# Last slab of the down weight gradient held back behind the last two row blocks, which are computed as a pair

## The chip, the cores and the metric

The kernel runs on one core of a Trainium2 chip. The metric is the device time of one execution in microseconds (us), shown as the median of several runs. A profile is one execution recorded by the hardware profiler. Its engines are called PE (TensorE, matrix products) and PEld (its weight loads), DVE (VectorE), ACT (ScalarE), POOL (GpSimd) and SP (SyncE, which only issues transfers). The execution with the profile has a time of its own, and within it a span from the first instruction to the last.

## The reference

The reference is the forward pass and all gradients of one block of a network. With x of 2048 rows and 1024 columns:

```python
x = A_q
xn = _layernorm(x, axis=-1)
s = _A_ref(xn, A_k, A_v, A_shift_k, A_ssm_k, A_ssm_D)       # xn * (long convolution of (shifted k) * v)
g = _silu(_B_ref(xn, B_w_gate, B_w_up, B_w_down))           # ((xn wg) * (xn wu)) wd
return x + s * g
```

`_A_ref` shifts k by four taps, multiplies by v, convolves along the 2048 rows by Fourier transforms and multiplies by its first argument. `_B_ref` has two projections from 1024 to 3584 columns, their product h, and one projection back, w_down, from 3584 to 1024. The outputs are this sum and the gradients for A_q, A_k, A_v, the taps, the convolution's kernel and its skip weights, w_gate, w_up and w_down. Two of them matter here. The gradient of w_down is h transposed times DBM, where DBM is the gradient behind the projection back; it is 3584 x 1024. The gradient of x (out_1) is the gradient of the two projections, DGU times the transposed w_gate and w_up, plus the part DXNA that comes through the convolution branch, taken back through the layer norm, plus grad_out.

## The kernel before

All products are in bf16 with sums in PSUM. The rows are tiled in 16 blocks of 128 (NB = 16), the 3584 columns in 14 slabs of 256 (NSL = 14). The kernel goes through stages, one after another on PE:

1. Layer norm, the two projections, h (written to DRAM as Hd) and the forward convolution.
2. The projection back and the gate for each row block, which writes DBM, DXNA and DY, the gradient for the convolution, to DRAM.
3. For each slab, the product dh (`dh_half`, L1189) and the weight gradients of w_gate and w_up (`dw_slab`, L1213). The product dgu goes to DRAM as DGd.
4. The gradient of w_down, slab by slab (the loop at L1293, products at L1320): for each slab two halves f of 128 rows, for each half two halves dh of 512 columns, and for each of those 16 matmuls over the row blocks. ACT copies the sums into `wbs` and SP stores it at L1325. The slabs of h are loaded by `load_h` (L1232) into three buffers in turn (HSL, L1247); DBM lies in U10, U8, U4 and U5 (L1246).
5. The gradient of x ("the dx stage", L1340 to L1429). Each row block sums 14 pieces n, 7 of w_gate and 7 of w_up, each of 8 matmuls of 128x512 (`dx_part`, L1340). A piece needs a transposed weight piece WGU[n] (1 MB, `load_wgu`, L1278) and, for each group g of four row blocks, a transposed tile dgut n (0.5 MB in two transfers, `load_dgut`, L1283). Group 0 runs as four row blocks at once, piece by piece; groups 1 to 3 as pairs, but for the last two row blocks, which run one after the other, the last of them in two halves of 512 columns (`parts = 2`, L1422). Behind each row block `ln_backward` (L1360) takes the sums back through the layer norm on DVE and ACT and stores the rows.

Two chains of vector work run beside the matmuls as generators. A pump takes steps from them: each step announces its weight with `yield`, and the pump goes on while the sum of the weights behind it is below the share of the stage that is done. `conv_backward` (L906) is pumped through stages 3 and 4 by `btick` (L1177), and begins with `dy_forward` (L885), which loads DYd by POOL, yields its first weight (L897) and then makes the first transforms on PE (`cmm`, L232). Its share is (bcnt - 10) / 410 of C_TOTAL (L1060); each dh group of 16 matmuls adds 1 to bcnt, each group of a weight gradient 2. What is left is run at once at slab 11 (`bdrain`, L1303). `dk_units` (L1006), the gradient of k and of the taps, is pumped through stage 5 by the count of `dx_part` calls (L1347): 16 units, each with a dkh load on POOL, and two transposed loads kT and dkT (L1020, L1022) on SP, for which each buffer exists once.

The order of the instructions on each engine and queue is set when the kernel is built, by a planner that goes by program order among what it estimates to be ready. With PIN set, the DVE's instructions keep program order. `tc.issue_after(ins)` puts what is issued inside behind `ins` on the same queue: the loads of the later dx pieces (L1387 to L1391) stand behind the last store of stage 4, `wst`. `ld` (L60) issues on SP, `st` and `cld` (L65) on POOL. A queue issues in order; a transfer that waits holds back those behind it.

Of the kernel before, what the change touches and what calls it, by code (L numbers as in the profile page):

```python
# [10 lines left out]
ACT = mybir.ActivationFunctionType  # L11
# [8 lines left out]
def build_kernel(  # L20
# [864 lines left out]
    def dy_forward(xs_, sp, cs, then):  # L885
        def load(ds):
            if ds < 8:
                cld(xs_[ds % 2], DYd[ds])

        def half(ds, i):  # L890
            if ds < 8:
                fwd8_half(xs_[ds % 2], i, sp[i], ps_c3)
            else:
                then[i]()
        load(0)
        load(1)
        yield 4.0  # L897
        half(0, 0)
        half(0, 1)
        for ds in range(8):  # L900
            load(ds + 2)
            X = cs.tile([P, 16, 256], BF16, name="DX")
            yield from fwd8(sp, X, cs, lambda i: half(ds + 1, i))
            st(DYFd[ds], X[:])
# [155 lines left out]
    C_TOTAL = 4.0 + 8 * FWD8_W + 16 * (PROD_W + INV8_W) + 8 * 1.4 + 8 * 2.5  # L1060
# [229 lines left out]

    flush()
    ts = []
    for k in range(NSL):  # L1293
        if k + 2 < NSL:
            load_h(k + 2)
# [16 lines left out]
        if k == 13:  # L1312
            ts.append(load_dgut(0, 5))
        h = hs.pop(k)
        for f in range(2):
            wbs = wo.tile([P, D], BF16, name="wbs")[:]
            for dh in range(2):
                ps = ps_b.tile([P, 512], F32, name="psb")
                for b in range(NB):
                    nc.tensor.matmul(ps[:], h[:, b, f * P:(f + 1) * P], DBM[b // 4][:, b % 4, dh * 512:(dh + 1) * 512],  # L1320
                                     start=(b == 0), stop=(b == NB - 1))
                nc.scalar.copy(out=wbs[:, dh * 512:(dh + 1) * 512], in_=ps[:])  # L1322
                btick(2)
            f0 = k * SLW + f * P
            wst = ld(o_dwd[f0:f0 + P, :], wbs)  # L1325
# [14 lines left out]
    def dx_part(t, i, ps, n, dhs=(0, 1)):  # L1340
        for f in range(4):
            for dh in dhs:
                nc.tensor.matmul(ps[:, dh * 512:(dh + 1) * 512], t[n][:, f, i * P:(i + 1) * P],  # L1343
                                 WGU[n][:, f, dh * 512:(dh + 1) * 512],
                                 start=(n == 0 and f == 0), stop=(n == 13 and f == 3))
        kcnt[0] += 1
        kpump(kcnt[0] / (14.0 * 14))  # L1347
# [3 lines left out]
    def ln_loads(b):  # L1351
        rows = slice(b * P, (b + 1) * P)
        ts_ = []
        for nm_, src in (("dxna_t", DXNAd), ("xn_t", XNd), ("dout_t", grad_out.flatten_outer_dims())):
            t = gl.tile([P, D], BF16, name=nm_, bufs=1)
# [4 lines left out]
    def ln_backward(b, mm, parts=1):  # L1360
# [3 lines left out]
        dxn = gl.tile([P, D], F32, name="dxn", bufs=1)  # L1364
        prod = gl.tile([P, D], F32, name="prod", bufs=1)
        dx_t = gl.tile([P, D], BF16, name="dx_t", bufs=1)
        cols = [slice(h * D // parts, (h + 1) * D // parts) for h in range(parts)]
        sums = gs.tile([P, 2, 2], F32, name="sums")
        for h, cl in enumerate(cols):
            ps = mm(h)  # L1370
            tt(dxn[:, cl], ps, dxna_t[:, cl], ADD)
            nc.scalar.activation(dx_t[:, cl], dxn[:, cl], ACT.Identity, accum_out=sums[:, 0, h:h + 1])  # L1372
            tt(prod[:, cl], dxn[:, cl], xn_t[:, cl], MUL)
            nc.scalar.activation(dx_t[:, cl], prod[:, cl], ACT.Identity, accum_out=sums[:, 1, h:h + 1])
        if parts == 2:
            tt(sums[:, :, 0], sums[:, :, 0], sums[:, :, 1], ADD)
        negm = gs.tile([P, 2], F32, name="negm")
        pinned(V.tensor_scalar(negm[:], sums[:, :, 0], -1.0 / D, None, op0=MUL))
        for cl in cols:
            nc.scalar.activation(prod[:, cl], xn_t[:, cl], ACT.Identity, bias=negm[:, 0:1], scale=negm[:, 1:2])  # L1380
            tt(dxn[:, cl], dxn[:, cl], prod[:, cl], ADD)
            pinned(V.scalar_tensor_tensor(dx_t[:, cl], dxn[:, cl], RSTN[:, b:b + 1], dout_t[:, cl], op0=MUL, op1=ADD))
            if parts == 1:
                ln_loads(b + 1)
            (st if parts == 1 else ld)(out_1.flatten_outer_dims()[rows, cl], dx_t[:, cl])

    for n in range(6, 14):  # L1387
# [11 lines left out]
    for i in range(4):  # L1399
# [5 lines left out]
        with tc.high_priority(40):  # L1405
            ln_backward(i, lambda h: pss[i][:])
    for g in range(1, 4):
        for b in (4 * g, 4 * g + 2):
            if b == NB - 2:
                break  # L1410

            pss = [ps_x.tile([P, D], F32, name="psx") for i in range(2)]
            for n in range(14):
                for i in range(2):
                    dx_part(ts, b % 4 + i, pss[i], n)
                if b % 4 == 2:
                    ts[n] = load_dgut(g + 1, n)
            for i in range(2):
                with tc.high_priority(40):
                    ln_backward(b + i, lambda h: pss[i][:])  # L1420
    for b in (NB - 2, NB - 1):
        parts = 2 if b == NB - 1 else 1  # L1422

        def mm(h):
            ps = ps_x.tile([P, D], F32, name="psx")
            for n in range(14):
                dx_part(ts, b % 4, ps, n, (h,) if parts == 2 else (0, 1))
            return ps[:, h * 512:(h + 1) * 512] if parts == 2 else ps[:]
        ln_backward(b, mm, parts)  # L1429
    kdrain()  # L1430
# [65 lines left out]
```

## Time and profile before

| | us |
|---|---|
| median of 11 runs | 1982.79 |
| lowest and highest of them | 1971.18, 2000.29 |
| the profiled execution's time | 1970.73 |
| its span | 1968.6 |
| its PE, DVE, ACT, POOL busy | 1936.3, 1511.7, 647.9, 359.7 |
| stage 4, up to its last matmul | about 1571.5 |
| dx stage, first to last matmul | 1572.1 to 1959.1 |

A busy time is the sum of an engine's instructions and not a limit by itself: what ends the span is the chain of waits. A row of the chain or of a timeline has a start, a length in us, the engine, the written tile, the line and a count. A row of the waits reads: who waited, for whom, us in total, times, the longest. A row of windows gives the stretch, its length, the busy time of PE, PEld, DVE, ACT and POOL with counts, the granted PE clock as a share of full speed, the share of the DMA engines and GB/s. SPq in a timeline is SP issuing a transfer, not the transfer itself. The time of one matmul in a list (379 ns for 128x512) includes its passage through the array, in which the next one overlaps.

### The profile page before, as it was taken

Reading aid. Unit: us, or ns where it says so; the run is one execution under the profiler, and the core shown is the slowest. Engines: PE = TensorE matmul, PEld = TensorE weight load, DVE = VectorE, ACT = ScalarE, POOL = GpSimd, SP = SyncE. Lnnn points to the kernel's source line nnn. Section 1 sums busy time; section 2 is a strip of 40 time slices with the busy share of each in tenths; the row PEclk is TensorE's granted clock in tenths of the full one; section 3 lists DMA queues with packets and bytes.
Section 4 is the critical chain, followed back from the end, with each engine's and each line's share of the span. In section 5 each row is a group of like instructions: output and inputs, shape, how many; then the busy total and the mean of one; then the engine's idle time right before and its main releaser. Section 6 shows DMA issues by size and latency. Waiting matters only on the chain.

```text
span 1968.6 us, 27524 instructions
## 1 busy us (share of the span) xinstructions
PE 1936.3 (98%) x11084; PEld 1041.9 (53%) x11084; DVE 1511.7 (77%) x1687; ACT 647.9 (33%) x954; POOL 359.7 (18%) x526
## 2 busy tenths in 40 slices
PE   7999999999999999999999999999999999999998
PEld 4455555555544446666566666664444444444443
DVE  8689999999626555888899889999996341566764
ACT  5665555555432223333222222222222100211113
POOL 3322213211212221000122112021121100111111
PEclk9999999999999999999999999999999999999999
DMA  7885857666799989565778899566796989989992
GB/s 262 272 269 200 284 198 242 202 213 220 256 292 304 280 264 300 203 208 203 257 231 266 181 276 311 203 241 213 163 302 161 158 191 199 211 168 182 187 167 70
DMA packets 452095, 443.37 MB, mean 225 GB/s; under 512 B 282624, under 2 KB 370488, under 8 KB 438144
## 3 DMA queue, kind: packets, MB, share of 16 engines
q1 hardware_dynamic: 390976, 228.93, 46.3%
q0 software_dynamic: 44672, 183.33, 29.2%
q10 hardware_dynamic: 16320, 29.36, 4.0%
q8 instruction: 86, 1.41, 0.3%
q14 instruction: 41, 0.34, 0.0%
HBM read 192.96 MB, written 189.83 MB: 194 GB/s over the span
## 4 chain that ended last, share of the span: by engine, by line
PE 77%; DVE 10%; issue 7%; DMA 2%; POOL 2%; ACT 1%; SPq 0%; POOLq 0%; DVEq 0%; ACTq 0%
PE psx L1343 20%; PE psb L1217 19%; PE psg L610 10%; PE psb L1320 10%; PE psb L1200 9%; PE psbm L1069 3%; PE psF L232 3%; DVE W L210 2%; DVE KX L210 2%; DVE U L210 2%; DVE HX L210 1%; DVE m L210 1%; PE psY L445 1%; PE psY L997 1%; PE psY L434 1%
## 5 line engine op out<-in xcount | busy, mean ns | idle before, releaser
L610 PE MATMUL psg<-wslab,U 128*128 128x512 bf16 x1792 | 409.3, 380 | 4.4 <-ACT gut L612 2.6
L1217 PE MATMUL psb<-U,U 128*128 128x512 bf16 x1792 | 397.2, 379 | 0.0
L1343 PE MATMUL psx<-U,dgut 128*128 128x512 bf16 x1536 | 333.2, 379 | 0.7 <-ACT wbs L1322 0.7
L1343 PEld LDWEIGHTS <-dgut 128*128 128x128 bf16 x1792 | 175.3, 98 | 212.4 <-issue 1.0
L1217 PEld LDWEIGHTS <-U 128*128 128x128 bf16 x1792 | 175.2, 98 | 197.7
L610 PEld LDWEIGHTS <-U 128*128 128x128 bf16 x1792 | 172.7, 98 | 193.1 <-issue 8.2
L1200 PE MATMUL psb<-wdt,U 128*128 128x256 bf16 x1792 | 206.3, 273 | 1.1 <-ACT bm L1087 1.1
L1320 PE MATMUL psb<-U,U 128*128 128x512 bf16 x896 | 194.4, 379 | 0.0
L1200 PEld LDWEIGHTS <-U 128*128 128x128 bf16 x1792 | 175.6, 98 | 32.1 <-issue 1.4
L612 ACT CAST gut<-psg 128x512 bf16<-128x512 f32 x216 | 126.4, 586 | 181.9 <-PE psg L610 178.8
L1069 PE MATMUL psbm<-U,ht 128*128 128x512 bf16 x784 | 169.9, 379 | 0.0
L1222 ACT CAST wb<-psb 128x512 bf16<-128x512 f32 x112 | 65.6, 586 | 312.0 <-PE psb L1217 301.0
L210 DVE TENSOR_TENSOR W<-W 128x1024 f32<-128x1024 f32 (+1 forms) x144 | 145.9, 1031 | 3.0
L1320 PEld LDWEIGHTS <-U 128*128 128x128 bf16 x896 | 87.5, 98 | 104.5
L1372 ACT ACTIVATE dx_t<-dxn 128x1024 bf16<-128x1024 f32 (+1 forms) x17 | 17.1, 1007 | 328.5 <-DVE dxn L210 243.7
L1069 PEld LDWEIGHTS <-ht 128*128 128x128 bf16 x784 | 76.6, 98 | 91.8
L210 DVE TENSOR_TENSOR U<-U,dht 128x2048 bf16<-128x2048 bf16 x56 | 68.3, 1221 | 50.3 <-ACT dht L1202 50.2
L1202 ACT CAST dht<-psb 128x512 bf16<-128x512 f32 x112 | 65.7, 586 | 120.3 <-PE psb L1200 118.0
L1048 DVE SCALAR_TENSOR_TENSOR dkp<-dkT,kT 128x1024 bf16<-128x1024 bf16 (+2 forms) x64 | 78.3, 1224 | 17.4 <-DMA dkT<-DKSHd 15.6
L1322 ACT CAST wbs<-psb 128x512 bf16<-128x512 f32 x56 | 32.8, 586 | 159.6 <-PE psb L1320 146.9
L210 DVE TENSOR_TENSOR W<-SP 128x1024 f32<-128x1024 f32 x64 | 74.3, 1218 | 6.0 <-ACT SP L254 5.3
L210 DVE TENSOR_TENSOR HX<-W 128x1024 bf16<-128x1024 f32 x64 | 74.9, 1218 | 0.4
(216 smaller groups left out, 2327.0 us busy)
## 6 DMA issues: line engine op xcount, KB each, us to landing
U<-GUd SPq DMA_DIRECT2D x28, 1024.0 KB, 8.7
DGd<-U SPq DMA_DIRECT2D x28, 1024.0 KB, 4.6
GUd<-gut ACTq DMA_DIRECT2D x54, 512.0 KB, 5.7
out_dram<-wb SPq DMA_DIRECT2D x112, 128.0 KB, 4.4
U<-Hd SPq DMA_DIRECT2D x14, 1024.0 KB, 5.9
Hd<-hN POOLq DMA_DIRECT2D x54, 256.0 KB, 4.7
HTd<-hT POOLq DMA_DIRECT2D x54, 256.0 KB, 4.1
ht<-HTd SPq DMA_DIRECT2D x7, 1536.0 KB, 9.5
```

Of the source, the lines that this page charges most:

```text
L210: pinned(V.tensor_tensor(o, a, b, op))
L232: mm = nc.tensor.matmul(ps[:, k].rearrange("p (c d) -> p c d", c=2), T[:, r, k, :], xr[:, r], start=(n == 0), stop=(n == len(rs) - 1 and ( ...
L610: gu_mm[0] = nc.tensor.matmul(ps[:], XNT[q][:, dc, qi * P:(qi + 1) * P], w[:, dc].rearrange("p a f -> p (a f)"), start=(dc == 0), stop=(dc ...
L612: nc.scalar.copy(out=gut[:, :, i], in_=ps[:].rearrange("p (a f) -> p a f", a=2))
L1048: ins = V.scalar_tensor_tensor(prod[:].rearrange("p r d -> p (r d)")[:, lo:H], dkT[:, 0, lo:H], 1.0, kT[:, 0, 13 + m + lo:13 + m + H], op0 ...
L1069: nc.tensor.matmul(ps[:, dh * 512:(dh + 1) * 512], ht(fc)[:, i * P:(i + 1) * P], WD[fc // 4][:, fc % 4, dh * 512:(dh + 1) * 512], start=(f ...
L1200: nc.tensor.matmul(ps[:, x * SLW:(x + 1) * SLW], DBMT[2 * hf + g][:, dc, (b % 4) * P:(b % 4 + 1) * P], wdt[:, dc, :], start=(dc == 0), sto ...
L1202: nc.scalar.copy(out=dht[:, 2 * e:2 * e + 2].rearrange("p b f -> p (b f)"), in_=ps[:])
L1217: nc.tensor.matmul(ps[:], XN[b // 4][:, b % 4, dc * P:(dc + 1) * P], dgus[b // 8][:, :, b % 8], start=(b == 0), stop=(b == NB - 1))
L1222: nc.scalar.copy(out=wb[:, dc % 2].rearrange("p a f -> p (a f)"), in_=ps[:])
L1320: nc.tensor.matmul(ps[:], h[:, b, f * P:(f + 1) * P], DBM[b // 4][:, b % 4, dh * 512:(dh + 1) * 512], start=(b == 0), stop=(b == NB - 1))
L1343: nc.tensor.matmul(ps[:, dh * 512:(dh + 1) * 512], t[n][:, f, i * P:(i + 1) * P], WGU[n][:, f, dh * 512:(dh + 1) * 512], start=(n == 0 and ...
```

## The change

Stage 4 ends after slab 12, and the 13th is computed at the very end. The last two row blocks run as a pair like the others, with twelve pieces together, then pieces 12 and 13 for one block and for the other, and the layer norm of each behind them. While this pair runs, DBM is loaded again into buffers that its pieces 0 to 3 leave, the last slab of h into the buffer of piece 4, and the inputs of the last layer norm into tiles of dgut that are free. The last layer norm has tiles of its own in the places of dgut 0 to 5 (`own`). Then come the 64 matmuls of slab 13, into PSUM tiles of the dx stage and `wbs` tiles in the places of the dk units' tiles, which are therefore run to their end first (`kdrain`); each half of 512 columns is stored by SP as soon as it is copied. The dk pump's share is counted over 13 row blocks instead of 14. The loads of dgut 5, which were issued at slab 13 of stage 4, go into the loop behind `wst`. `ln_backward` no longer has a form in two parts, and its output tile has two buffers. Apart from that, the first weight of `dy_forward` is 7.0 instead of 4.0, also in C_TOTAL.

```diff
--- before.py
+++ after.py
@@ -894,7 +894,7 @@
                 then[i]()
         load(0)
         load(1)
-        yield 4.0
+        yield 7.0
         half(0, 0)
         half(0, 1)
         for ds in range(8):
@@ -1057,7 +1057,7 @@
         st(o_dshk.rearrange("(c p) j -> p c j", p=P), dsko[:])
     DK_TOTAL = 3 + 16 * 7
 
-    C_TOTAL = 4.0 + 8 * FWD8_W + 16 * (PROD_W + INV8_W) + 8 * 1.4 + 8 * 2.5
+    C_TOTAL = 7.0 + 8 * FWD8_W + 16 * (PROD_W + INV8_W) + 8 * 1.4 + 8 * 2.5
     bpump, bdrain = make_pump(conv_backward(), C_TOTAL)
 
     ddo = const.tile([P, 8], BF16, name="ddo")
@@ -1288,10 +1288,15 @@
             nc.sync.dma_start_transpose(out=t[:, 2 * i:2 * i + 2], in_=DGd[2 * j + i, a, 512 * g:512 * g + 512, :])
         return t
 
+    def dwd_mm(ps, h, f, dh):
+        for b in range(NB):
+            nc.tensor.matmul(ps, h[:, b, f * P:(f + 1) * P], DBM[b // 4][:, b % 4, dh * 512:(dh + 1) * 512],
+                             start=(b == 0), stop=(b == NB - 1))
+
     flush()
     ts = []
-    for k in range(NSL):
-        if k + 2 < NSL:
+    for k in range(NSL - 1):
+        if k + 2 < NSL - 1:
             load_h(k + 2)
         with tc.issue_after(wst.ins) if k > 0 else nullcontext():
             if k in (2, 3, 4, 5, 6):
@@ -1309,16 +1314,12 @@
         if k == 12:
             load_wgu(6, gw.tile([P, 4, D], BF16, name="W1")[:])
             ts.append(load_dgut(0, 4))
-        if k == 13:
-            ts.append(load_dgut(0, 5))
         h = hs.pop(k)
         for f in range(2):
             wbs = wo.tile([P, D], BF16, name="wbs")[:]
             for dh in range(2):
                 ps = ps_b.tile([P, 512], F32, name="psb")
-                for b in range(NB):
-                    nc.tensor.matmul(ps[:], h[:, b, f * P:(f + 1) * P], DBM[b // 4][:, b % 4, dh * 512:(dh + 1) * 512],
-                                     start=(b == 0), stop=(b == NB - 1))
+                dwd_mm(ps[:], h, f, dh)
                 nc.scalar.copy(out=wbs[:, dh * 512:(dh + 1) * 512], in_=ps[:])
                 btick(2)
             f0 = k * SLW + f * P
@@ -1337,14 +1338,14 @@
     kpump, kdrain = make_pump(dk_units(kw_), DK_TOTAL)
     kcnt = [0]
 
-    def dx_part(t, i, ps, n, dhs=(0, 1)):
+    def dx_part(t, i, ps, n):
         for f in range(4):
-            for dh in dhs:
+            for dh in range(2):
                 nc.tensor.matmul(ps[:, dh * 512:(dh + 1) * 512], t[n][:, f, i * P:(i + 1) * P],
                                  WGU[n][:, f, dh * 512:(dh + 1) * 512],
                                  start=(n == 0 and f == 0), stop=(n == 13 and f == 3))
         kcnt[0] += 1
-        kpump(kcnt[0] / (14.0 * 14))
+        kpump(kcnt[0] / (14.0 * 13))
 
     ln_in = {}
 
@@ -1352,39 +1353,39 @@
         rows = slice(b * P, (b + 1) * P)
         ts_ = []
         for nm_, src in (("dxna_t", DXNAd), ("xn_t", XNd), ("dout_t", grad_out.flatten_outer_dims())):
-            t = gl.tile([P, D], BF16, name=nm_, bufs=1)
+            t = gl.tile([P, D], BF16, name=nm_, bufs=1) if b < NB - 1 else own(nm_, BF16, len(ts_))
             cld(t[:], src[rows, :])
             ts_.append(t)
         ln_in[b] = ts_
 
-    def ln_backward(b, mm, parts=1):
+    def own(nm_, dt, n):
+        return (gd2 if n < 4 else gd).tile([P, D], dt, name=nm_ + "l", tag=f"dgut{n}")
+
+    def ln_backward(b, ps):
 
         rows = slice(b * P, (b + 1) * P)
         dxna_t, xn_t, dout_t = ln_in.pop(b)
-        dxn = gl.tile([P, D], F32, name="dxn", bufs=1)
-        prod = gl.tile([P, D], F32, name="prod", bufs=1)
-        dx_t = gl.tile([P, D], BF16, name="dx_t", bufs=1)
-        cols = [slice(h * D // parts, (h + 1) * D // parts) for h in range(parts)]
-        sums = gs.tile([P, 2, 2], F32, name="sums")
-        for h, cl in enumerate(cols):
-            ps = mm(h)
-            tt(dxn[:, cl], ps, dxna_t[:, cl], ADD)
-            nc.scalar.activation(dx_t[:, cl], dxn[:, cl], ACT.Identity, accum_out=sums[:, 0, h:h + 1])
-            tt(prod[:, cl], dxn[:, cl], xn_t[:, cl], MUL)
-            nc.scalar.activation(dx_t[:, cl], prod[:, cl], ACT.Identity, accum_out=sums[:, 1, h:h + 1])
-        if parts == 2:
-            tt(sums[:, :, 0], sums[:, :, 0], sums[:, :, 1], ADD)
+        if b < NB - 1:
+            dxn = gl.tile([P, D], F32, name="dxn", bufs=1)
+            prod = gl.tile([P, D], F32, name="prod", bufs=1)
+            dx_t = gl.tile([P, D], BF16, name="dx_t", bufs=2)
+        else:
+            dxn, prod, dx_t = own("dxn", F32, 3), own("prod", F32, 4), own("dx_t", BF16, 5)
+        sums = gs.tile([P, 2], F32, name="sums")
+        tt(dxn[:], ps, dxna_t[:], ADD)
+        nc.scalar.activation(dx_t[:], dxn[:], ACT.Identity, accum_out=sums[:, 0:1])
+        tt(prod[:], dxn[:], xn_t[:], MUL)
+        nc.scalar.activation(dx_t[:], prod[:], ACT.Identity, accum_out=sums[:, 1:2])
         negm = gs.tile([P, 2], F32, name="negm")
-        pinned(V.tensor_scalar(negm[:], sums[:, :, 0], -1.0 / D, None, op0=MUL))
-        for cl in cols:
-            nc.scalar.activation(prod[:, cl], xn_t[:, cl], ACT.Identity, bias=negm[:, 0:1], scale=negm[:, 1:2])
-            tt(dxn[:, cl], dxn[:, cl], prod[:, cl], ADD)
-            pinned(V.scalar_tensor_tensor(dx_t[:, cl], dxn[:, cl], RSTN[:, b:b + 1], dout_t[:, cl], op0=MUL, op1=ADD))
-            if parts == 1:
-                ln_loads(b + 1)
-            (st if parts == 1 else ld)(out_1.flatten_outer_dims()[rows, cl], dx_t[:, cl])
-
-    for n in range(6, 14):
+        pinned(V.tensor_scalar(negm[:], sums[:], -1.0 / D, None, op0=MUL))
+        nc.scalar.activation(prod[:], xn_t[:], ACT.Identity, bias=negm[:, 0:1], scale=negm[:, 1:2])
+        tt(dxn[:], dxn[:], prod[:], ADD)
+        pinned(V.scalar_tensor_tensor(dx_t[:], dxn[:], RSTN[:, b:b + 1], dout_t[:], op0=MUL, op1=ADD))
+        if b < NB - 2:
+            ln_loads(b + 1)
+        st(out_1.flatten_outer_dims()[rows, :], dx_t[:])
+
+    for n in range(5, 14):
         with tc.issue_after(wst.ins):
             if n > 6:
                 load_wgu(n, u8((6, 3, 11, 10, 8, 4, 5)[n - 7], a=4))
@@ -1403,31 +1404,41 @@
             for n in (12, 13):
                 ts[n] = load_dgut(1, n)
         with tc.high_priority(40):
-            ln_backward(i, lambda h: pss[i][:])
+            ln_backward(i, pss[i][:])
     for g in range(1, 4):
         for b in (4 * g, 4 * g + 2):
-            if b == NB - 2:
-                break
-
+            end = b == NB - 2
             pss = [ps_x.tile([P, D], F32, name="psx") for i in range(2)]
-            for n in range(14):
+            for n in range(12 if end else 14):
                 for i in range(2):
                     dx_part(ts, b % 4 + i, pss[i], n)
-                if b % 4 == 2:
+                if end and n < 4:
+                    DBM[n] = u8((7, 0, 1, 9)[n], a=4)
+                    ld(DBM[n], DBMd[512 * n:512 * n + 512, :].rearrange("(b u) d -> u b d", u=P))
+                if end and n == 4:
+                    h = u8(2, "p (b f) -> p b f", b=NB)
+                    ld(h, Hd[NSL - 1])
+                if end and n == 8:
+                    ln_loads(NB - 1)
+                if b % 4 == 2 and not end:
                     ts[n] = load_dgut(g + 1, n)
+            if end:
+                kdrain()
             for i in range(2):
+                if end:
+                    for n in (12, 13):
+                        dx_part(ts, b % 4 + i, pss[i], n)
                 with tc.high_priority(40):
-                    ln_backward(b + i, lambda h: pss[i][:])
-    for b in (NB - 2, NB - 1):
-        parts = 2 if b == NB - 1 else 1
-
-        def mm(h):
-            ps = ps_x.tile([P, D], F32, name="psx")
-            for n in range(14):
-                dx_part(ts, b % 4, ps, n, (h,) if parts == 2 else (0, 1))
-            return ps[:, h * 512:(h + 1) * 512] if parts == 2 else ps[:]
-        ln_backward(b, mm, parts)
-    kdrain()
+                    ln_backward(b + i, pss[i][:])
+    for f in range(2):
+        ps = ps_x.tile([P, D], F32, name="psx")
+        wbs = kw_.tile([P, D], BF16, name="wbs", tag=("dka", "dkp")[f])
+        f0 = (NSL - 1) * SLW + f * P
+        for dh in range(2):
+            hs_ = slice(dh * 512, (dh + 1) * 512)
+            dwd_mm(ps[:, hs_], h, f, dh)
+            nc.scalar.copy(out=wbs[:, hs_], in_=ps[:, hs_])
+            ld(o_dwd[f0:f0 + P, hs_], wbs[:, hs_])
     for p_ in (ps_x, kw_, gs, gl, gd2, ub, ua, gd, gw):
         p_.release()
 
```

## The prediction

> **What bounds the kernel now.** The page comes first: TensorE is busy almost throughout, so only its idle time and the work behind its last matmul can be won.
>
> ```profile
> PE 1936.3 (98%) x11084; PEld 1041.9 (53%) x11084; DVE 1511.7 (77%) x1687; ACT 647.9 (33%) x954; POOL 359.7 (18%) x526
> ```
>
> The chain that ended last, read from 1500 us on, gives the rate and the tail (columns: start, length, what).
>
> ```profile
> 1572.12 387.02 PE psx L1343 x1792
> 1959.14 0.02 issue
> 1959.16 0.70 DVE dxn L210
> ...
> 1964.79 0.75 DVE dx_t L1382
> ```
>
> The dx stage is one unbroken run: 387.02 / 1792 = 0.216 us a matmul. After its end at 1959.14 the layer norm of the last row block stands alone, then a store, up to the span's end at 1968.6: 9.46 us without a matmul.
>
> The waits of TensorE between 770 and 1530 us, and the windows around the one they hold, show the second loss.
>
> ```profile
> PE psF L232 <- DMA A<-DYd: 3.2, 1, 3.2
> 776.00:780.00 4.00, 3.92 (x22) 2.93 (x22) 0.87 (x1) 2.13 (x3) 0.00 (x0) 0.59 0.81 305
> ```
>
> The reader sees one wait of 3.16 us for the first load of DYd (it ended at 776.08) and a granted clock of 0.59 over the next 4 us, which loses 0.41 x 4 = 1.6 us more.
>
> Last, SP's queue from 1523 to 1660 us and the weight loads' waits from 1640 to 1700 us. This is where the moved slab stands now.
>
> ```profile
> 1535.45 22.39 SPq L1288 DMA_TRANSPOSE dgut<-DGd  x3
> 1558.09 1.67 SPq L1020 DMA_TRANSPOSE kT<-in_A_k_dram  x1
> 1560.43 1.22 SPq L1022 DMA_TRANSPOSE dkT<-DKSHd  x1
> ...
> 1578.62 1.16 SPq L1020 DMA_TRANSPOSE kT<-in_A_k_dram  x1
> 1579.83 1.29 SPq L1022 DMA_TRANSPOSE dkT<-DKSHd  x1
> 1581.21 0.53 SPq L61 DMA_DIRECT2D out_dram<-wbs  x1
> ...
> 1591.84 0.57 SPq L61 DMA_DIRECT2D out_dram<-wbs  x1
> 1592.52 2.65 SPq L1288 DMA_TRANSPOSE dgut<-DGd  x2
> 1595.21 11.75 SPq L1281 DMA_TRANSPOSE U<-in_B_w_up_dram  x1
> ...
> 1651.73 8.95 SPq L1288 DMA_TRANSPOSE dgut<-DGd  x6
> ```
> ```profile
> PEld L1343 <- DMA dgut<-DGd: 0.4, 1, 0.4
> ```
>
> The loads of the dx stage (pieces 6 to 13) start only at 1592.52, because SP's queue holds the slabs' stores behind kT loads, which wait for DVE. The 13th piece came 0.4 us late (TensorE went on at 1657.65). So this stream has no slack today, and nobody sees it because slab 13 covers its first 13.8 us.
>
> **Part 1: the slab moves.** 2 x 2 x 16 = 64 matmuls, 64 x 0.216 = 13.8 us, leave the place between the slabs and the dx stage and come back behind it: sum 0. Its Hd load (1 MB) moves too, and the four DBM pieces (1 MB each) are loaded a second time. In the last pair a piece takes 2 x 8 x 0.216 = 3.46 us, so these five are released 3.5 to 17.3 us into the pair and needed 48.4 us in (14 x 3.46). A Hd load lands in 5.7 us (median; 21.7 at worst here): hidden, with 9 us over at the worst; without that cover one load costs 5.7. No transposes are then queued on SP: the pump is finished at 13 row blocks instead of 14, and DVE had finished its last step of it at 1921.1, right behind that count.
>
> **Part 2: the end.** Now: 9.46. Then: after the last matmul an ACT copy of 128x512 (0.59), about 0.05 to start the store, 1.7 for its landing (the SP stores of dx_t, 128 KB, median), 1.3 from that landing to the span's end (1967.28 to 1968.6): 3.7. The layer norms must fit beside the slab. A full one took 7.8 (1921.01 to 1928.79). DVE's order is pinned, so that of block 15 runs behind that of block 14: 15.6 after block 14's sums, and its POOL store lands 3.1 to 3.4 after issue: some 19.2. The slab's last store lands 3.46 + 13.8 + 0.65 + 1.7 = 19.6 after the same point. The two nearly tie; I take the slab, and leave 1 us for the other. ACT's copies queue behind the norms' activations, but each of the slab's two tiles has its own PSUM buffer, so no matmul waits. **Gain 5.8, bounds 4.8 and 6.0.**
>
> **Part 3: first step 7.0 instead of 4.0.** The backward pump stands at bcnt 14 when it now takes the first transform (4 x 636.8/410 = 6.2 > 4). With 7.0 it needs bcnt 15 (5 x 639.8/410 = 7.8). Between lies one group of 16 dh matmuls of 128x256: half of the 32 that the chain gives 3.49, so 1.75. The load itself is issued by POOL at 763.44 behind a store, and does not move. The wait shrinks from 3.16 to 1.4. The clock: waits of 2.6 at L610 and 1.1 at L1200 are in the list of waits, and the granted clock stays at 1.0 there, so I take it that 1.4 does not lower it: 1.6 more. **Gain 3.35; bounds 1.75 (the clock drops anyway) and 4.8 (the wait goes wholly).** DVE does not take it back: the last inverse transform's input was ready at 1509.6 and TensorE took it at 1521.15, 11.6 later.
>
> The Trainium skill (TensorE: Matmul & The Clock Gate, HAM oscillation — how this bites in real kernels) asks for no idle gaps above about 3.4 us. The 0.59 behind a wait of 3.16 disagrees; by the page the drop would not come from this wait, and the part would be worth 1.75, the sum 7.5.
>
> **Part 4: the start of the dx stage.** TensorE needs every piece 13.8 earlier. Piece 5 goes from before the kT loads into the stream: 2.65 longer. Before: 1657.65 - 1592.52 = 65.1 from the stream's start to the last piece. Needed at 1657.26 - 13.8 = 1643.4, so the stream must start by 1643.4 - 65.1 - 2.65 = 1575.7; if the first weight load, 11.75, takes the 4.3 to 5.6 of its sisters, by 1582.7. When does it start? SP's order behind piece 4: kT and dkT of unit 0, two stores, kT and dkT of unit 1, a store, kT and dkT of unit 2, slab 12's last store. The two transposes of piece 5, 7.36 of the 22.39 above, are gone, so dkT issues at 1560.43 - 7.4 = 1553.0 and lands 3.2 later; unit 0's four products take 5.05 (1563.66 to 1568.7), unit 1 takes 10.0 (1568.6 to 1578.6), then 3.2 as now until the store is out: 1553.0 + 3.2 + 5.05 + 10.0 + 3.2 = 1574.5. That is 1.2 before the limit. **Cost 0.** Bounds: a gain of 0.4 (today's late piece); a loss, if the stream starts as late as now, of 1592.5 - 1575.7 = 16.8. The nearest row is the queue's order itself, so I take 0.
>
> The Trainium skill (DMA: Bandwidth & Descriptors, Latency and other measured facts) gives DMA transposes 261 GB/s: an estimate of 6.0 us for a piece of 1.5 MB. Measured: six pieces from 1607.00 to 1651.73, 7.45 each, against TensorE's 6.9; by the page the stream would win 0.9 a piece and leave part 4 with 10 us of slack, the sum unchanged.
>
> **Sum.** 5.8 + 3.35 + 0 = 9.1 us, against the profiled execution's 1970.73: 1961.6. That execution lies 12.1 below the median of the runs shown; I carry the difference over: 1982.8 - 9.1 = 1973.7. From the rows I cannot say where the other runs lose their 12; a stretch like 1536 to 1549, where the DMA queues moved 10 GB/s on average, is a candidate, and the Hd load of slab 13 landed 21.7 after 1535.02, at 1556.7, 0.9 before its matmuls began.
>
> **Rivals.**
> - *The stream comes late (the other side).* At the start of the dx stage TensorE waits for a piece. Price: start minus 1575.7. With one more kT unit ahead it is 1584.5: 8.9, and the sum is -0.2, no change. With the start of now it is 16.8, plus 1.6 of lowered clock as behind the wait at 772.9: 9.3 slower, 1992. It decides from a start at 1584.8 on, 9.1 later than the limit. For it: no slack today, transposes that crawl. Against: two transposes fewer ahead of the chain, one kT unit fewer before the last store.
> - *More is gained.* Slab 13's narrow Hd load and today's late pieces cost the usual run more than the profiled one; both are relieved. 5.8 + 4.8 + 0.4 = 11.0, and up to 5.7 more for a Hd load that misses: 1966 to 1972. For it: the 12 us between profile and median. Against: no row shows that wait.
> - *Part 3 does nothing.* POOL's load lands later, or the transform keeps its place: only 5.8, 1977. For it: the load's landing is decided by DMA traffic. Against: it is issued by the same queue at the same point.
>
> **How the numbers follow.** The measurement of this kernel tells about 0.5% (9.9 us) from no change, and the sum lies just inside it. Sum case 0.41, split by its bounds (6.6 to 11.2) in half: 0.21 faster, 0.20 same. More gained 0.19, faster. Part 3 nothing 0.12, same. Late stream 0.28: 0.13 same, 0.15 slower. Together faster 0.40, same 0.45, slower 0.15. The likeliest case's own range is 1971 to 1977; the range of 8 in 10 goes from 1964 (all of the second rival, and 2 us more for the two medians' own spread) to 1992 (the first rival).
>
> **What would show it.** The last matmul ends some 3.7 us before the span's end and belongs to the slab; a copy and an SP store follow. The wait for A<-DYd is about 1.4, and no window behind it shows a clock under 0.9. The first store-then-transpose of the dx stream lies about 16.9 us after the last slab's matmuls (1574.5 against 1557.6); no wait for dgut or U appears in the dx stage. Wrong: a wait of several us on dgut or U, a POOL store that ends the span, kT loads between the last slab store and its forerunner, or slower transposes.

## The result, and the profile after

The change made the kernel slower: a median of 1999.28 us over 12 runs (1985.18 to 2004.99) against 1981.26 over 47 runs of the kernel before, a ratio of 1.0088, 95% interval 1.0067 to 1.0108. By the ratio that is 17 us lost, where 9 had been forecast as won.

The profiled execution of after took 2003.48 us, its span is 2001.7; against the 1968.6 of before the two spans differ by 33.1. The profile of after lies 4.2 above its median and that of before 10.5 below its own, so the two traces show the loss larger than it usually is. The working below accounts for the 33.1, and the experiments put a price with an interval on the cause.

The page of after, its row of engines and its row of TensorE in 40 slices of 50 us:

```profile
PE 1944.7 (97%) x11084; PEld 1042.4 (52%) x11084; DVE 1510.9 (75%) x1682; ACT 646.6 (32%) x949; POOL 355.5 (18%) x527
...
PE   7999999999999999999999999999999985999999
```

TensorE has as many matmuls as before and is busy 8.4 us longer, and two slices, from some 1600 to 1700 us, now have holes. The waits of TensorE over the whole span of after name what it waited for there:

```profile
PE psx L1344 <- DVE dxn L210: 22.8, 2, 17.3
PE psx L1344 <- DMA dgut<-DGd: 6.3, 5, 4.6
...
PE psF L232 <- DMA A<-DYd: 4.0, 1, 4.0
```

The largest is new in kind. Two times, 17.3 and 5.5 us, the dx stage stood still for DVE to read the sums of a row block out of PSUM into `dxn` (after's timeline of TensorE from 1640 to 1715 us; in brackets: idle before, and what ended it):

```profile
1651.71 14.69 PE L1344 MATMUL psx<-U,dgut 128*128 128x512 bf16 x56 [4.62 <-DMA dgut<-DGd]
1683.71 3.57 PE L1344 MATMUL psx<-U,dgut 128*128 128x512 bf16 x8 [17.31 <-DVE dxn L210]
1692.78 18.01 PE L1344 MATMUL psx<-U,dgut 128*128 128x512 bf16 x72 [5.50 <-DVE dxn L210]
```

Group 0 holds four of these PSUM tiles, and the first pair of group 1 needs two of them back. What DVE did in that time, in after's timeline of DVE from 1585 to 1700 us:

```profile
1589.71 0.69 DVE L210 TENSOR_TENSOR dka<-dka,dkp 128x1024 bf16<-128x1024 bf16 x1
1675.35 1.23 DVE L1048 SCALAR_TENSOR_TENSOR dkp<-dkT,kT 128x1024 bf16<-128x1024 bf16 x1 [84.95 <-DMA dkT<-DKSHd]
...
1682.44 1.22 DVE L210 TENSOR_TENSOR dxn<-psx,dxna_t 128x1024 f32<-128x1024 f32 x1
...
1691.51 1.22 DVE L210 TENSOR_TENSOR dxn<-psx,dxna_t 128x1024 f32<-128x1024 f32 x1
```

DVE was idle for 84.95 us. It waited for the transposed load dkT of the fourth dk unit (unit 3, counted from 0). Its order is pinned, and in that order unit 3 comes ahead of the layer norms of group 0, so their first read of PSUM stood at 1682.44 behind a load that had nothing to do with them. In before the same read came as soon as TensorE had the sums, with only the last of unit 3's products behind it (before's timeline of DVE from 1655 us):

```profile
1658.78 1.22 DVE L210 TENSOR_TENSOR dxn<-psx,dxna_t 128x1024 f32<-128x1024 f32 x1 [61.06 <-PE psx L1343]
...
1666.53 1.22 DVE L1048 SCALAR_TENSOR_TENSOR dkp<-dkT,kT 128x1024 bf16<-128x1024 bf16 x1
```

Why the load was late is in SP's queue, after's timeline of SP from 1520 to 1720 us:

```profile
1572.63 1.16 SPq L1020 DMA_TRANSPOSE kT<-in_A_k_dram  x1
1573.88 1.25 SPq L1022 DMA_TRANSPOSE dkT<-DKSHd  x1
1575.18 1.04 SPq L61 DMA_DIRECT2D out_dram<-wbs  x2
1576.27 9.24 SPq L1288 DMA_TRANSPOSE dgut<-DGd  x4
1585.61 11.91 SPq L1281 DMA_TRANSPOSE U<-in_B_w_up_dram  x1
...
1647.99 22.15 SPq L1288 DMA_TRANSPOSE dgut<-DGd  x16
1670.24 1.24 SPq L1020 DMA_TRANSPOSE kT<-in_A_k_dram  x1
1671.54 1.48 SPq L1022 DMA_TRANSPOSE dkT<-DKSHd  x1
```

The loads of units 0, 1 and 2 are ahead of the stream of the dx stage, that of unit 3 is behind it, and behind seven dgut tiles of group 1 as well (16 transfers, of which the first two are group 0's last tile): it is issued at 1670.24, 94 us behind the stream's start at 1576.27. In before unit 3's kT was issued just ahead of the stream's start at 1592.52 (before's timeline of SP):

```profile
1588.72 1.16 SPq L1020 DMA_TRANSPOSE kT<-in_A_k_dram  x1
```

Standing still also cost clock. After's windows over the gap and over the rest of the dx stage:

```profile
1640.00:1710.00 70.00, 42.30 (x165) 17.13 (x164) 26.16 (x34) 10.62 (x15) 6.81 (x12) 0.78 1.01 201
1710.00:1983.00 273.00, 273.00 (x1266) 123.77 (x1265) 168.35 (x234) 40.33 (x58) 42.32 (x71) 1.00 0.76 167
```

The 165 matmuls of the first window take 42.30 us instead of 165 x 0.216 = 35.6, with a granted clock of 0.78 on average: 6.7 more. By the timeline of TensorE above, some 2.5 of it stand behind the wait of 4.62 for dgut (56 matmuls in 14.69 us instead of 12.1), the rest behind the two waits for dxn.

The end of after is as the change means it to be; its chain that ended last:

```profile
1692.78 290.82 PE psx L1344 x1336
1983.61 10.37 PE psx L1293 x48
...
1994.64 3.63 PE psx L1293 x16
...
1998.29 0.58 ACT wbs L1440
```

The last matmul ends at 1998.25 and the span at 2001.7, 3.45 later, where before had 9.46. Between the two rows of slab matmuls lie 0.67 us for the copy of an earlier tile. The end thus wins 9.46 - 3.45 - 0.67 = 5.3.

Put together: the dx stage starts at 1558.99 instead of 1572.12 (13.1 earlier: the 13.8 of slab 13, less 0.7 that the way up to it lost). It takes 424.5 instead of 387.0, 37.4 more: 22.8 for dxn, 6.3 for dgut, 6.7 of clock, and 1.6 that is left over, about what the stage loses to small waits of weight loads before 1646 us. From its last matmul to the span's end it is 18.3 instead of 9.5, 8.8 more, which is the slab and its wait less the 6.0 at the end. -13.1 + 37.4 + 8.8 = 33.1.

### The profile page after: what moved, and what is told of

Its sections match the earlier page's. It is cut to its first block, busy times and chain, and to the rows that moved or that the text cites. A ratio compares the mean times of both kernels' runs of the same rounds, so it can differ in the third digit from the quotient of the medians.

```text
span 2001.7 us, 27536 instructions
## 1 busy us (share of the span) xinstructions
PE 1944.7 (97%) x11084; PEld 1042.4 (52%) x11084; DVE 1510.9 (75%) x1682; ACT 646.6 (32%) x949; POOL 355.5 (18%) x527
## 5 line engine op out<-in xcount | busy, mean ns | idle before, releaser
L1217 PE MATMUL psb<-U,U 128*128 128x512 bf16 x1792 | 397.4, 379 | 0.0
L1344 PE MATMUL psx<-U,dgut 128*128 128x512 bf16 x1536 | 341.0, 384 | 30.1 <-DVE dxn L210 22.8
L1293 PE MATMUL psb<-U,U 128*128 128x512 bf16 x832 | 180.6, 379 | 0.0
L1376 ACT ACTIVATE dx_t<-dxn 128x1024 bf16<-128x1024 f32 x15 | 15.9, 1057 | 363.9 <-DVE dxn L210 234.9
```

The lines of the kernel that those rows point to most:

```text
L1217: nc.tensor.matmul(ps[:], XN[b // 4][:, b % 4, dc * P:(dc + 1) * P], dgus[b // 8][:, :, b % 8], start=(b == 0), stop=(b == NB - 1))
L1293: nc.tensor.matmul(ps, h[:, b, f * P:(f + 1) * P], DBM[b // 4][:, b % 4, dh * 512:(dh + 1) * 512], start=(b == 0), stop=(b == NB - 1))
```

## The experiments

Three theories stood after this, and a fourth, D, comes with its run. A: DVE's pinned order holds the norms behind unit 3, whose load the stream has overtaken on SP; without that, the other terms of the prediction's sum hold. B: the stream itself is late (dgut), which is the rival on record, and the wait for dxn only follows. C: the pump's new divisor, 13 row blocks instead of 14, brings unit 3 forward in DVE's order. The short diffs are against after, unless another kernel is named; all ratios are against before on the same chip, with 95% intervals.

**Unit 3 held behind the norms.** The pump may not begin unit 3 until the four row blocks of group 0 are through. Loads keep their order on SP, and only DVE's order changes.

```diff
-        kpump(kcnt[0] / (14.0 * 13))
+        part = kcnt[0] / (14.0 * 13)
+        kpump(min(part, 24.0 / DK_TOTAL) if kcnt[0] <= 56 else part)
```

> The changed kernel, with one condition more on the dk pump: it stands still at 24 (behind unit 2) until the four layer norms of group 0 are issued, so that unit 3 stands behind them in DVE's order instead of ahead. Theory A (DVE's fixed order: unit 3 waits for its kT and dkT, which SP now issues behind the dx stream and eight pieces of the next group, and the four norms, whose first read frees the sums' buffers, wait behind unit 3): TensorE's wait for dxn, 22.8 us in the changed kernel's profile, falls under 2, the two low stretches of the clock behind it go too, and the kernel is 0.2 to 0.6% faster than before. Theory B (the stream of transposed loads is what is late; the wait for dxn only follows from it): the waits for dgut grow instead and the time stays 0.6 to 0.9% above before. Theory C (the dk pump counted over 13 row blocks brings too much vector work into the stage): some gain, but the wait for dxn stays over 8 us, since the units are only shifted.

0.9957 (0.9934 to 0.9979), a median of 1967.0. The waits of TensorE in this kernel from 1540 us to the end:

```profile
PE psx L1344 <- ACT wbs L1323: 0.7, 1, 0.7
PE psx L1293 <- ACT wbs L1441: 0.7, 1, 0.7
```

Both waits of the dx stage are gone, and its window has no hole and no lowered clock:

```profile
1563.00:1961.00 398.00, 397.29 (x1840) 180.03 (x1840) 230.24 (x320) 58.29 (x84) 55.53 (x93) 1.00 0.86 187
```

SP still issues unit 3's kT behind the stream, at 1667.62, about where after had it. DVE reads the first sums at 1649.99, when TensorE has them (this kernel's timelines of DVE and of SP):

```profile
1649.99 1.23 DVE L210 TENSOR_TENSOR dxn<-psx,dxna_t 128x1024 f32<-128x1024 f32 x1 [61.75 <-PE psx L1344]
```
```profile
1667.62 1.51 SPq L1020 DMA_TRANSPOSE kT<-in_A_k_dram  x1
```

So the late load alone costs nothing that shows here; what costs is that the norms stand behind it. Theory B falls with this run as the main cause: the stream starts 17.8 us behind the dx stage's first matmul (1581.26 against 1563.46), no earlier than in after (17.3), and TensorE doesn't wait for it. The first four dgut transfers and the first weight piece took SP 7.29 and 6.30 us here, against 9.24 and 11.91 in after; why they went faster stays open. So the wait for dgut is gone here as well as that for dxn, and the price holds both. It is the difference of the two ratios, 1.0088 - 0.9957 = 1.31% or 26 us, and with the two intervals' half widths of 0.20 and 0.23 taken together, sqrt(0.20^2 + 0.23^2) = 0.30%, between 20 and 32 us.

**The old divisor.** One count back to 14 x 14, for theory C.

```diff
-        kpump(kcnt[0] / (14.0 * 13))
+        kpump(kcnt[0] / (14.0 * 14))
```

> The changed kernel with the dk pump counted over 14 row blocks again; unit 3 then stands with three of its four products ahead of the first norm on DVE, and its loads still behind the stream on SP. Theory A: no help, TensorE's wait for dxn stays at 15 to 25 us, 0.5 to 0.9% slower than before. Theory C (the faster pump is the cause): the wait goes, and the time comes to 0 to 0.5% faster than before. Theory B: as A, with the waits for dgut unchanged.

1.0085 (1.0056 to 1.0113), not to be told from after. The waits of TensorE in this kernel:

```profile
PE psx L1344 <- DVE dxn L210: 20.8, 2, 15.1
PE psx L1344 <- DMA dgut<-DGd: 5.0, 2, 4.5
```

The same two waits stand there. C falls: the old share also begins unit 3 before the norms.

**No dk unit before the norms at all.** The pump starts only behind group 0, so no kT load stands ahead of the stream.

```diff
-        kpump(kcnt[0] / (14.0 * 13))
+        if kcnt[0] > 56:
+            kpump((kcnt[0] - 56) / (14.0 * 14 - 56))
```

> The changed kernel with no dk unit pumped before the four norms of group 0; the 16 units are spread over the rest. SP then has one kT and dkT ahead of the dx stream instead of three, with no wait for DVE between the slabs' stores. Theory A: no wait for dxn in group 0, the stream starts at about 1560 instead of 1576 and no wait for dgut is left in group 0; 0.2 to 0.7% faster than before, if DVE carries 16 units (160 us) and 12 norms in the 250 us that are left; if it doesn't, waits for dxn come up in groups 1 to 3. Theory B: the gain comes from the waits for dgut alone, that is 11 us at most. Theory C: worse than the changed kernel, since the pump runs denser later.

0.9960 (0.9928 to 0.9991). The stream started at 1553.51, 1.5 us after the dx stage's first matmul, and no wait for dxn or dgut is left. The end paid for it. TensorE's waits and the window of the last part of this kernel:

```profile
PE psx L1293 <- ACT wbs L1441: 7.0, 2, 6.3
```
```profile
1945.00:1966.00 21.00, 12.60 (x44) 4.85 (x43) 9.00 (x10) 9.19 (x14) 2.54 (x4) 0.82 0.25 75
```

DVE has all the dk work behind group 0, is busy 179.70 us of the 245 from 1700 to 1945 (162.62 in the kernel of the first experiment), and reaches the norms of the last row blocks later: it reads the sums of block 14 at 1943.83, 5.1 us behind the slab's first matmul, where in the first experiment it reads them 3.3 us ahead of it. The slab's first copy on ACT (at 1948.94) stands behind the activations of that norm, and the slab's next matmuls wait 6.3 us for it. It is the same pattern at another engine: what stands in front in a fixed order makes the rest late. The stream 23 us earlier than in after brings no time that can be told from the first experiment's, with this loss at the end in it.

**Unit 3 ahead of the stream.** The other way to feed DVE: the load of unit 3 goes in front of the stream again (`dk_ld[0]` is the dkT load that was issued last).

```diff
+    kpump(25.0 / DK_TOTAL)
     for n in range(5, 14):
-        with tc.issue_after(wst.ins):
+        with tc.issue_after(dk_ld[0].ins):
```

> The changed kernel with DVE's order as it is, but unit 3's kT and dkT ahead of the whole dx stream on SP (the stream stands behind them instead of behind slab 12's last store). Theory A: the wait for dxn goes, as unit 3 finds its data; the stream starts about 10 us later than in the changed kernel, near 1586, so TensorE waits about 10 us in all for dgut or U in group 0; the time is within 0.3% of before. Theory B: worse than the changed kernel, by about the 10 us that the stream starts later. Theory C: the wait for dxn stays.

1.0000 (0.9974 to 1.0025). The wait for dxn is gone (the first norm read at 1654.20), but the stream starts at 1586.94, 10.1 us later than the 1576.84 at which its last slab store goes out, and TensorE pays that:

```profile
PE psx L1346 <- DMA dgut<-DGd: 7.6, 6, 5.0
```

Here is the rival "the stream comes late" by itself: 0.43% or 8.5 us against the first experiment, between 2 and 15 by the two intervals. The prediction had priced one more kT unit ahead at 8.9. The run also parts the price above. In its profile the waits for dgut are as long as after's (7.6 against 6.3), that for DYd is 3.5 shorter, and the wait for dxn is gone. Against after it wins 1.0088 - 1.0000 = 0.88% or 17 us, between 11 and 24, and most of this belongs to the wait for dxn and the clock behind it.

**Before, with the stream let loose one slab earlier.** This run is set against theory D: that slab 13 is missing as a cover, so that TensorE comes to the stage before its data. Against before: slab 13 and the old end stay in place, and only the anchor of the stream moves to the last store of slab 12 (`wst12`).

```diff
-        with tc.issue_after(wst.ins):
+        with tc.issue_after(wst12.ins):
```

> The kernel before with one edit: the dx stream stands behind the last store of slab 12 instead of slab 13's. Slab 13 stays in its place, so TensorE has its cover, and the end is the old one. On SP the kT and dkT of unit 3 then come behind the stream and five pieces of group 1. Theory A (the order of SP's queue against DVE's fixed order): slower in spite of the earlier stream; unit 3 gets its data near 1667, the norms follow near 1671, and TensorE, which needs the first sums' buffer at 1669, waits 8 to 14 us for dxn in two pieces, with a lowered clock; 0.4 to 0.8% slower. Theory D (the slab that is gone as a cover is the cause, since TensorE comes to the stage 13.8 us before its data): no wait for dxn, and 0 to 0.2% faster, since the stream starts 10 us earlier.

1.0072 (1.0043 to 1.0101). TensorE's waits in this kernel and DVE's timeline:

```profile
PE psx L1345 <- DVE dxn L210: 12.8, 2, 7.4
```
```profile
1671.25 1.23 DVE L1048 SCALAR_TENSOR_TENSOR dkp<-dkT,kT 128x1024 bf16<-128x1024 bf16 x1 [77.04 <-DMA dkT<-DKSHd]
...
1674.94 1.22 DVE L210 TENSOR_TENSOR dxn<-psx,dxna_t 128x1024 f32<-128x1024 f32 x1
```

Nothing of the change is in this kernel but the place of the stream ahead of unit 3's loads (kT at 1665.99), and it loses 14 us in the same way, with 0.6 us of waiting for dgut in its profile. D falls as the cause, since the cover is there. An earlier stream is a loss as long as unit 3 falls behind it and the norms behind unit 3.

**Before, with slab 13 left out.** Against before: the last 256 rows of the w_down gradient are not computed, and nothing takes their place at the end. Its load of h is left out too (not in this short diff).

```diff
+        if k == NSL - 1:
+            break
         h = hs.pop(k)
```

> The kernel before with slab 13 left out: the last 256 rows of the gradient of w_down aren't computed, 64 matmuls or 13.8 us less work on TensorE, and the old end. SP's order is then that of the changed kernel, with unit 3 behind eight pieces of group 1. Theory A: the wait for dxn appears (15 to 25 us in two pieces and 4 to 7 us of lowered clock), so that it is 0.2 to 0.8% slower than before in spite of the work left out. If slab 13's place meant nothing, it would be 0.7% faster.

1.0074 (1.0047 to 1.0100). With 13.8 us less work on TensorE the kernel takes 15 us more. Its waits of TensorE:

```profile
PE psx L1345 <- DVE dxn L210: 20.2, 2, 14.9
PE psF L232 <- DMA A<-DYd: 6.0, 1, 6.0
PE psx L1345 <- DMA dgut<-DGd: 5.8, 4, 4.6
```

Taking the slab away from its place is enough for the loss. The new end, its reloads and its pair are not needed for it.

**The hold in before, a control.** Against before, the same hold of unit 3, with its own 14 x 14 in the share.

> A control: the kernel before, with unit 3 of the dk pump held behind the four norms. Theory A says that nothing is won by it here, since in the kernel before unit 3's loads stand ahead of the stream and it never held up the norms; but holding it also takes one kT and dkT, and its wait for DVE, from SP's queue ahead of the last slab's store, so that the stream starts about 10 us earlier: 0 to 0.2% faster. If holding unit 3 is good in itself (and not only where its loads are late), 0.4% or more.

0.9996 (0.9973 to 1.0019). The stream did not start earlier, which had been expected: the planner put unit 3's kT ahead of it all the same (1587.48, the stream at 1591.28). So the hold brings nothing of its own where the norms do not stand behind a late load, and what the first experiment won over after is the loss taken back.

**The first weight.** Three runs for part 3 of the prediction: 4.0 and 13.0 in the kernel with the hold, and 13.0 alone in before (in C_TOTAL as well).

```diff
-        yield 7.0
+        yield 13.0
```

> The changed kernel with unit 3 held behind the norms, and the first weight of the backward pump back at 4.0. Theory of the forecast's part 3: TensorE comes to the first transform 1.75 us earlier after the issue of its load (about 9.6 instead of 11.4 us) and waits that much longer, up to 3.4 us with the clock: 0 to 0.2% slower than the same kernel with 7.0, so 0.2 to 0.5% faster than before. Rival: the wait is set by where the load lands, 11 to 19 us after its issue in the profiles so far, and the difference is lost in that.

> The changed kernel with unit 3 held behind the norms, and the first weight 13.0: the first transform stands 18 to 19 us behind the issue of its load instead of 11.4. Expected: no wait for A<-DYd in the profile, or under 1 us, the chain of the last inverse transform still ready before TensorE takes it, and 0.3 to 0.7% faster than before. If the vector work of this stage were tight, TensorE would wait for it at slab 10 or 11 instead.

> The kernel before with one edit: the first weight of the backward pump 13.0 instead of 4.0. The first transform moves behind the landing of its load, so the wait for A<-DYd (3.2 in the kernel before's profile, 4.0 to 7.5 in others) and the low clock behind it (1.6 to 3.4) go. Expected: 0.15 to 0.5% faster than before. If the wait is rare outside the profiled executions, no difference.

With 4.0: 0.9974 (0.9942 to 1.0005). With 7.0, above: 0.9957 (0.9934 to 0.9979). With 13.0: 0.9932 (0.9912 to 0.9952). In before alone: 0.9972 (0.9954 to 0.9989). The first two can't be told apart, nor the second and the third by their intervals: the profile of 4.0 has a wait of 5.8 for the load of DYd, and that of 7.0 one of 7.5. With 13.0 both profiles have none, and in before that is worth 0.28%, 5.5 us. The reason lies in the landings. POOL issues this load at 762 to 765 us in all of them, and it landed 12.6 us later in before, 15.4 in after and 18.7 in the kernel with the hold. In the other profiles that waited for it, it landed between 9.3 and 15.5 us after the issue. With 7.0 TensorE arrives 11.2 to 11.4 us after the issue, ahead of all three; with 13.0 it arrives 17.9 after.

The run with the hold and 13.0 had a wait in the dx stage again, with a lowered clock behind it (this kernel's waits, and its window behind that wait):

```profile
PE psx L1344 <- DMA dgut<-DGd: 2.5, 1, 2.5
```
```profile
1643.00:1647.00 4.00, 4.00 (x12) 1.31 (x11) 0.89 (x1) 0.00 (x0) 0.00 (x0) 0.57 1.03 187
```

**Both, with the hold one unit earlier.** To have the stream start earlier, the hold is put at 17.0, before unit 2.

```diff
-        kpump(min(part, 24.0 / DK_TOTAL) if kcnt[0] <= 56 else part)
+        kpump(min(part, 17.0 / DK_TOTAL) if kcnt[0] <= 56 else part)
```

> The changed kernel with units 2 and 3 held behind the norms and the first weight 13.0. One kT and dkT fewer stand ahead of slab 12's last store, so the dx stream starts near 1562 to 1567 instead of 1575, and the wait for dgut in group 0 (2.5 us in the version with unit 3 alone held) goes; 0.6 to 0.9% faster than before. If the units that are left then crowd DVE, waits for dxn show in groups 1 to 3 or at the last slab.

0.9933 (0.9905 to 0.9961), a median of 1961.96 (1960.12 to 1971.47): not to be told from the run above, and with it the fastest. It beats both kernels of the case, after by 1.0088 / 0.9933 - 1 = 1.6%. The stream started at 1571.15, not at the 1562 to 1567 expected: unit 2's load still went out ahead of the last slab's store (1567.51). The waits of TensorE in this kernel, from 700 us to the end, are down to three short ones:

```profile
PE psb L1200 <- ACT bm L1087: 1.1, 1, 1.1
PE psx L1344 <- ACT wbs L1323: 0.7, 1, 0.7
PE psx L1293 <- ACT wbs L1441: 0.7, 1, 0.7
```

Two buffers for kT and dkT, which would let SP load unit 3 early without a wait for DVE, were not tried.

## Why the prediction was wrong, point by point

**Part 1, the slab's move at cost 0: right.** After's slab at the end waited for none of its five reloads; its only wait is the 0.67 for ACT's copy. The prediction had none there ("so no matmul waits"); in the run with no dk unit before the norms these waits came to 7.0.

**Part 2, the end: right.** 5.8 had been predicted with bounds of 4.8 and 6.0; 5.3 came. The near tie of the last norm and the slab's store was also there: the dx_t of block 15 was finished 15.5 us after block 14's first read of its sums (predicted 15.6), and its store was issued at 1995.95, while the slab's last store ended the span.

**Part 3, the first weight: right in mechanism, mis-sized by its landing.** TensorE reached the transform at 774.35, 11.36 us after the load's issue at 762.99, where in before it was 9.48: 1.9 later, for a predicted 1.75. The load landed at 778.40, 15.4 after its issue instead of 12.6, so the wait was 4.0, not 1.4, and the clock of the 4 us behind it 0.66. The term that failed is that the load "does not move": it is issued at the same place, but a landing is no constant. In three other profiles with 7.0 the wait was 1.0 (old divisor), 0.5 (unit 3 ahead of the stream) and nothing (no dk unit before the norms). The rival "part 3 does nothing" is what this profile shows, and a weight that has TensorE arrive 17.9 us after the issue is worth 5.5 us in before.

**Part 4, "Cost 0": the step that failed.** Its sum for the start of the stream was good: 1574.5 predicted, 1576.27 measured, against a limit of 1575.7. That start is 0.6 past the limit, and 6.3 of waiting for dgut came: from its start to the last piece the stream took 75.4 us (1576.27 to 1651.71), where 65.1 + 2.65 had been counted. The first weight load took 11.91 again, and the transfers before and after it were slow as well (9.24 and 8.37). This is the small part. The large one is that the step asked only whether TensorE would have its pieces in time. It counted that one kT unit fewer would stand ahead of the stream, put that down as evidence against the late stream, and did not ask what became of that unit: behind the stream its load comes some 80 us later, DVE waits for it, and DVE's pinned order has the norms of group 0 behind it. The same working had used that pinned order in part 2. The price is 20 to 32 us with the waits for dgut (from the first experiment) and 11 to 24 where these stay (from the run with unit 3 ahead of the stream), and the wait for dxn is neither in the sum nor in a rival.

**The rivals.** "The stream comes late" was the rival on the losing side; it named the right stage and a wait for the wrong thing. The two are opposite ends of one choice: with unit 3 ahead of the stream TensorE waits for dgut (1.0000), with unit 3 behind it and the norms behind unit 3 it waits for DVE (1.0088). Its bound of 1992 came from the first end alone, and the median lies above it. Of "more is gained", the wait for slab 13's load of h came up once and small: 1.5 us in the run with the stream let loose one slab earlier, where it landed 22.3 us after its issue; the profiles of before and of its other two variants that compute slab 13 have none.

**The rest of the sum.** With that one step repaired the change measures 0.9957, 8.5 us faster (4 to 13 by the interval), against a sum of 9.1. The agreement is partly luck: the profile of that run still has a wait of 7.5 for DYd, with a clock of 0.57 over the 12 us from 776 on, so part 3 had brought nothing there, and the end's 5.3 is most of it.

## What to carry to other kernels

When work is taken from in front of a stream of loads, two questions belong together: whether the consumer has its pieces in time, and what the stream now overtakes on its queue. For each load that is overtaken, find the engine that waits for it and read what stands behind that wait in the engine's fixed order, down to the PSUM buffers that this work would have freed. A margin for a load is taken from the spread of its landings over several profiles, not from one landing.

## What the runs showed of the hardware

A wait of 2.5 us can lower TensorE's clock, and need not. Behind the 2.5 us of the run with the hold and 13.0 the granted clock was 0.57 over the next 4 us and then 1.00 again; behind 3.16 us in before it was 0.59; behind 2.6 us at 81 us in before it stayed at 1.00 (84 to 88 us). The prediction took a wait of 1.4 us as free for the clock because 2.6 had been: 1.58 us in the control left it at 1.00 (774 to 778 us), but the row of 2.6 is no safe bound.

The Trainium skill (TensorE: Matmul & The Clock Gate, HAM oscillation — how this bites in real kernels) asks for no gaps above about 3.4 us. Here 2.5 was enough once, so the measurement decides against that bound. The same page (What's actually happening) says that the window in which the gate looks at activity runs freely, so where a gap lies in it would matter; that fits the two outcomes at 2.5 and 2.6 us, but no run here moved a gap to show it.

One dgut transfer, the second of piece 4, held SP for 12.17 to 14.36 us in after (13.66) and in all seven runs made from it, and 14.98 in before, while two of its sisters together mostly take 2.6. It comes back at the same place of the program; its cause was not looked for further and stays open. The landing of the DYd load, 9.3 to 18.7 us after the same instruction, is the other figure that no reading of one profile would have given.
